# Moving one bias addition and one pair's LayerNorm pieces within the MLP of an adaLN block

## The chip, the cores and the metric

The kernel runs on one core of one Trainium2 chip. The metric is the time of one execution on the device in microseconds; several executions are timed and their median is given. Beside them one execution is recorded by the hardware profiler; its times are microseconds from the start of its span. Five engines work side by side, each through its own queue of instructions in order: PE (matmul, with its weight loads as PEld), DVE (vector), ACT (scalar), POOL (GpSimd) and SP, which here only starts DMAs.

## The reference

One transformer block over 2048 tokens of 640 features. Six vectors are made from a condition `c`, then attention and MLP each act on a LayerNorm that these vectors scale and shift:

```python
mod = (silu(c) @ w_mod).reshape(1, 6, 1, -1)          # sa, ca, ga, sb, cb, gb
h = layernorm(x) * (1 + ca) + sa
x = x + ga * A(h)                                     # linear attention, 32 heads of 20
h = layernorm(x) * (1 + cb) + sb
r = relu(h @ w1 + b1)                                 # 640 -> 1728
x = x + gb * ((r * r) @ w2 + b2)                      # 1728 -> 640
```

Everything is float32. Matmuls are done as sums of products of a rounded part ("hi") and the rest ("lo").

## The kernel before

The tokens stand in 16 tiles of 128, two tiles to a pair, so that the MLP goes over eight pairs, j = 0 to 7. A pair has seven steps n of two half steps. I call the half steps by pair and number: 2:4 is pair 2, half step 4, which is n = 2, first half. This is also the number `at` that the tables `LN_AT...` use. Pair 3 is the fourth pair.

In half step j:k PE computes `up`: 128 of the 1728 hidden features for both tiles of the pair (L79, tile `up`). ACT adds `b1` and takes the relu into `ft` (L1268), DVE squares it (L1269), ACT and DVE make its hi and lo parts `ra` (L1292, L89). After `up` PE does its share of the products with `w2` for the step before (tiles `acc`, `acc3x`). From pair 2 on these products are done in a scheme with fewer products, for which DVE also makes four sums (L1283), split into `rs` (L1308), and which reads prepared weights from a `ring` of four tiles. POOL fetches these from HBM, one fetch for each product that frees a tile (`t_fetch`, L1378). The prepared weights are made during pairs 1 and 2: `t_load` loads two rows `traw`, `t_sums` subtracts, `t_split` splits and SP stores them; the sixth and last of these (`t_split(5)`, tile `tst_end`) stands in half step 2:5.

From pair 2 on both `up` outputs of a step lie in one PSUM bank, so the next `up` starts only once the relu of the one before has read its half. The last hidden chunk (half step 13) has 64 features, and DVE reads its half of the bank, too (L1273), then makes the square (L1274).

While PE works on pair j, the other engines prepare pair j + 1: `load_x1` loads `XM`, `ln_dealt` takes two sums (L1538) and two sums of squares (L1543) on ACT, with POOL's small operations after each two (L1540, L1545 to L1547); then copies of the statistics (L1555, L1557), the normalisation of a second, "dealt" copy `XX` of the tokens (L1562, loaded by eight small DMAs in `load_dealt`), DVE's transposes `turn` (L1104), and in `t2` (L374, L375, and a subtraction on DVE) the scaled and split `H2` for the next pair's `up`. At which half step each piece stands is written in the tables: `ln` has seven places (two sums, two sums of squares, the copies, two normalisations), `dealt` and `turn` are the loads and transposes, and the keys 9 to 13 are the parts of `t2`.

When a pair's products are done, the next pair's half steps 0 and 1 read them out (`end`, L1440), and `finish` adds the residual rows `XR` (L1437) and stores. `residual` loads `XR` at n = 5, and `add_bias` adds `gb * b2` to them, two additions of 128 x 640.

Rows of 640 floats come from a pool "s1" of five buffers; a new row waits until one of the five has been read for the last time. One is held to the end by the last piece of `w1`. The others serve `traw`, `XR`, and, for pair 3 alone, the dealt rows, because the buffer that other pairs use for them is taken:

```python
BUFS = {"k": 2, "s1": 5, "s2": 2, "s3": 3, "s4": 5}
places += [lambda nm: row("s1", nm)[:, None, :].bitcast(F32R)]
```

The order of instructions on PE, DVE, ACT and POOL is as the program is written within a pair's region (pairs 0, 1 and 2 to 7 are three regions); between regions, and on SP in pair 1, a planner sets the order.

Of the kernel before, what the change touches and what calls it, by code (L numbers as in the profile page):

```python
# [52 lines left out]
def kernel(  # L53
# [64 lines left out]
    def row(tag, name):  # L118
        return (pc if tag in ("s3", "s4") else mem).tile([P, D], F32, tag=tag, name=name, bufs=BUFS[tag])
# [598 lines left out]
    for t in range(2, NT - 2):  # L718
        j, i = divmod(t, 2)
# [341 lines left out]
    XX = {}  # L1061
# [26 lines left out]

    def load_dealt(j):
        if j == 3:  # L1090
            XX[j] = [row("s1", f"xx{j}_{i}") for i in range(3)]
        else:
            h = ht(f"xx{j}", j).rearrange("p d s n -> p (d s n)").bitcast(F32)
            XX[j] = [h[:, D * i : D * i + D] for i in range(3)]
        for i in range(2):
            for q in range(4):
                nc.sync.dma_start(
                    XX[j][i][32 * q : 32 * q + 32].rearrange("t (a c) -> t a c", a=4),
                    A1[2 * j + i][:, 160 * q : 160 * q + 160].rearrange("(a t) c -> t a c", a=4),
                )  # L1100
# [328 lines left out]
    def add_bias(j, i):  # L1429
        add(XR[j, i], XR[j, i], bb)  # L1430
# [5 lines left out]
    def add(o, a, b):  # L1436
        nc.vector.tensor_tensor(o, a, b, op=ALU.add)  # L1437

    def by_gate(o, a, c):
        nc.vector.tensor_tensor(o, a, gb_b[:, c], op=ALU.mult)  # L1440
# [14 lines left out]
    def end(j, r, i, c):  # L1455
        o = Y[j][i][:, c]
        if j >= PLAIN:
            add(o, o, acc(j, r)[1])
        else:
            by_gate(o, acc(j, r)[1], c)  # L1460
# [43 lines left out]

    LN_AT0 = {"load": 0, "dealt": 1, "ln": (2, 3, 3, 4, 5, 7, 8), "turn": (8, 9), 10: (0, 1), 11: (2, 3), 12: (4,)}
    LN_AT1 = {"load": 0, "dealt": 1, "ln": (2, 2, 3, 3, 4, 5, 7), "turn": (6, 8), 9: (0, 1), 11: (2, 3), 12: (4,)}
    LN_AT2 = {"load": 0, "dealt": 5, "ln": (5, 5, 6, 6, 7, 8, 9), "turn": (9, 10), 11: (0, 1), 12: (2, 3), 13: (4,)}
    LN_AT = {"load": 0, "dealt": 1, "ln": (4, 4, 5, 5, 6, 7, 8), "turn": (8, 9), 10: (0, 1), 11: (2, 3), 12: (4,)}
    PREPS = iter([1, 3] + [2, 1, 2, 2, 1, 2] + [1, 1] + [1, 2])

# [20 lines left out]
    def ln_dealt(j):  # L1531
        sm = small([P, 2], "sm", f"smb{j}")
        rn = tiny.tile([P, 2, 2], F32, tag="rn", name=f"rn{j}", bufs=1)
        ra = tiny.tile([P, 4, 2, 2], F32, tag="rna", name=f"rna{j}", bufs=1)
        sq, nb = rn[:, :, 0], rn[:, :, 1]
        junk = XX[j][2]
        for i in range(2):
            nc.scalar.activation(junk, XM[j][:, i], AF.Identity, accum_out=sm[:, i : i + 1])  # L1538
            if i:
                nc.gpsimd.tensor_scalar(sm, sm, -1.0 / D, None, op0=ALU.mult)  # L1540
            yield
        for i in range(2):
            nc.scalar.activation(junk, XM[j][:, i], AF.Square, bias=sm[:, i : i + 1], accum_out=rn[:, i, 0:1])  # L1543
            if i:
                nc.gpsimd.tensor_scalar(sq, sq, 1.0 / D, EPS, op0=ALU.mult, op1=ALU.add)  # L1545
                nc.gpsimd.tensor_tensor(sq, sq, mhalf, op=ALU.pow)
                nc.gpsimd.tensor_tensor(nb, sm, sq, op=ALU.mult)  # L1547
            yield
        for a in range(4):
            for q in range(4):  # L1550
                o, v = ra[32 * q : 32 * q + 32, a], rn[32 * a : 32 * a + 32]
                if j <= PLAIN:
                    nc.gpsimd.tensor_copy(o, v)
                elif q % 2:
                    nc.scalar.activation(o, v, AF.Copy)  # L1555
                else:
                    nc.vector.tensor_copy(o, v)  # L1557
        yield
        for i in range(2):
            for a in range(4):  # L1560
                x = XX[j][i][:, 160 * a : 160 * a + 160]
                nc.scalar.activation(x, x, AF.Identity, bias=ra[:, a, i, 1:2], scale=ra[:, a, i, 0:1])  # L1562
            yield

    def layer(j, at, part=None):
        todo = {1: LN_AT0, PLAIN: LN_AT1, PLAIN + 1: LN_AT2}.get(j, LN_AT)
        if j == NB:
# [21 lines left out]
    for j in range(NB):  # L1589
        if j <= PLAIN:  # L1590
            if j:
                by_hand.__exit__(None, None, None)
            by_hand = tc.manual_schedule(engines={ET_.PE, ET_.DVE, ET_.Activation, ET_.Pool} | ({ET_.SP} if j != 1 else set()))
            by_hand.__enter__()
        for n in range(NP):
            down = lambda k: prev and (down_plain if plain(*prev) else down_pair)(*prev, k)
            twice = not plain(j, n)
            m = NP * j + n - NP - 1
            if (j, n) == (NB - 1, NP - 1):
                for k in range(2):  # L1600
                    up(j, 2 * n + k)
                    split_a(j, n, (k,))
                break
            done = j - 1 if j and prev else None
            up(j, 2 * n)
            if prev and not plain(*prev):
                split_s(*prev)
            down(0)
            if j < PLAIN:
                layer(j + 1, 2 * n, None if j else 0)  # L1610
            if 0 < m < NP - 2:
                t_split(m - 1)
            if m == -1:
                t_load(0)
            if (j, n) == (PLAIN, 0):
                t_fetch(4)
            if j >= PLAIN:
                if n == 5 + (j == PLAIN) - (j == NB - 1):
                    for i in range(2):
                        add_bias(j, i)  # L1620
                layer(j + 1, 2 * n)
            prep(next(PREPS, 0))
            if j == 0:
                layer(j + 1, 2 * n, 1)
            if n == 0 and j:
                if j - 1 >= PLAIN:
                    first_combos(j - 1)
                else:
                    Y[j - 1] = [row("s2", f"y{j - 1}_{i}") for i in range(2)]
                for r, i, c in (("3", 0, R), ("2", 0, L)):  # L1630
                    end(j - 1, r, i, c)
            if n == 1 and j:
                gate(j - 1, 0)
                if j != PLAIN:
                    finish(j - 1, j < PLAIN)
            if n == 1 and j == PLAIN:
                finish(j - 1, 0)
            if n == 2 and j == PLAIN:
                t_sums(NP - 2)
            if n == (2 if j > PLAIN else 1) and j:  # L1640
                gate(j - 1, 1)
            if n == (5, 5, 5, 3)[min(j, 3)]:
                residual(j)
            for i in range(2):
                if n == 6 and j == 0:
                    add_bias(j, i)
            if j == NB - 1 and n == 1:
                for k in range(NP - LAST, NP - 1):
                    plain_load(k)
            if j == NB - 1 and n == 3:  # L1650
                for k in range(NP - LAST, NP - 1):
                    plain_split(k)
            if j == NB - 1 and n == NP - 2:
                for i in range(2):
                    by_gate(Y[j][i], Y[j][i], slice(0, D))
                    add(Y[j][i], Y[j][i], XR[j, i])
            up(j, 2 * n + 1)
            if j >= PLAIN and n == 0:
                down(1)
            split_a(j, n)  # L1660
            if twice:
                sums(j, n)
            if j < PLAIN or n:
                down(1)
            if m == NP + 1:
                t_split(NP - 2)
            ahead = (j, n) == (0, 3)
            if ahead:
                layer(j + 1, 2 * n + 1)
            prep(next(PREPS, 0))  # L1670
            if n == 0 and j:
                end(j - 1, "4", 1, L)
                end(j - 1, "x", 1, R)
            if n == (2 if j > PLAIN else 1 if j == PLAIN else 0) and j:
                finish(j - 1, j >= PLAIN)
            if not ahead:
                layer(j + 1, 2 * n + 1)
            if (j, n) == (0, 4):
                nc.vector.tensor_tensor(bb, bb, gb_b, op=ALU.mult)
            if 0 <= m < NP - 2:  # L1680
                t_sums(m)
            if m == NP - 2:
                t_split(m - 1)
            if 0 < m + 1 < NP - 1:
                t_load(m + 1)
            if m == NP - 1:
                for i in range(2):
                    add_bias(j - 1, i)
            if j == NB - 1 and n == NP - LAST:
                first_combos(j)  # L1690
            prev = j, n
# [60 lines left out]
```

## Time and profile before

| | |
|---|---|
| median of 3 runs | 762.3 us (761.41 to 762.86) |
| profiled execution | 760.53 us, span 758.8 us |
| busy: PE, PEld, DVE, ACT, POOL | 751.5, 732.2, 605.3, 456.7, 168.7 us |
| granted TensorE clock | 1.000 |
| MLP | from about 387 us to the end |

A row of the timeline gives the start in us, the duration, the engine, the line of the program, the operation, output and input tiles with their shape, the number of instructions merged into the row, and in brackets the idle time of the engine ahead of it with what ended it. Starts are those of the first instruction of a row, and instructions on one engine can overlap a little.

### The profile page before, as it was taken

The page shows a single profiled execution, that of the slowest core. Times are in us where ns is not written, and L with a number is a line of the kernel's source. Part 1 is how long each engine was busy: PE and PEld are TensorE (multiplying, and loading weights), DVE is VectorE, ACT ScalarE, POOL GpSimd, SP SyncE. Part 2 cuts the span into 40 slices and gives each one's busy share as a digit, 9 for nine tenths or more (in the row PEclk, how much of TensorE's full clock was granted, in tenths as well). Part 3 has the DMA queues.
Part 4 walks back from the last instruction along what each step waited for, and adds up shares of the span by engine and source line. Part 5 has one row for each costly group of instructions (what it writes and reads, how often), then busy time and mean ns, then how long its engine had stood idle before and what let it go on. Part 6 is the DMA issues. An engine that isn't in the chain of part 4 may idle for free.

```text
span 758.8 us, 15386 instructions
## 1 busy us (share of the span) xinstructions
PE 751.5 (99%) x5898; PEld 732.2 (96%) x5898; DVE 605.3 (80%) x1121; ACT 456.7 (60%) x1054; POOL 168.7 (22%) x349
## 2 busy tenths in 40 slices
PE   9999999999999999999999999999999999999997
PEld 9999999999999988998999999999999999999997
DVE  6598997988999899998655868777777776777766
ACT  5767666677853365555777656466474756647431
POOL 3001101011100247543413020132221313213110
PEclk9999999999999999999999999999999999999999
DMA  9812431342332354644886555997677777767461
GB/s 328 329 57 83 139 105 54 105 137 103 137 105 94 94 167 149 164 105 105 208 206 213 141 191 212 283 273 214 186 206 209 205 196 201 207 177 216 125 182 36
DMA packets 57778, 126.04 MB, mean 166 GB/s; under 512 B 7324, under 2 KB 15265, under 8 KB 57705
## 3 DMA queue, kind: packets, MB, share of 16 engines
q1 hardware_dynamic: 37554, 78.75, 31.5%
q0 software_dynamic: 17568, 41.00, 21.9%
q10 hardware_dynamic: 2583, 5.30, 1.8%
q8 instruction: 46, 0.75, 0.4%
q14 instruction: 27, 0.22, 0.1%
HBM read 100.29 MB, written 29.89 MB: 172 GB/s over the span
## 4 chain that ended last, share of the span: by engine, by line
PE 87%; DVE 9%; ACT 3%; issue 1%; POOL 0%; DVEq 0%; POOLq 0%
PE up L79 22%; PE acc L79 16%; PE pq L79 9%; PE pk L79 9%; PE pv L79 9%; PE pwo L79 6%; PE acc3x L79 4%; PE kvp L455 3%; PE te L925 1%; DVE dn L883 1%; DVE scr L881 1%; DVE ezb L905 1%; PE ta L363 1%; DVE ot L89 1%; PE foldq L281 1%
## 5 line engine op out<-in xcount | busy, mean ns | idle before, releaser
L79 PE MATMUL up<-h,w 128*128 128x256 f32 x1640 | 204.6, 277 | 1.2 <-ACT ft L1268 0.9
L79 PEld LDWEIGHTS up<-h,w 128*128 128x128 f32 x1640 | 196.3, 188 | 2.1 <-ACT ft L1268 1.2
L1268 ACT ACTIVATE ft<-up,b_t 128x256 f32<-128x256 f32 x104 | 48.8, 470 | 97.4 <-PE up L79 97.2
L79 PE MATMUL acc<-w,ra 128*128 128x384 f32 x452 | 97.9, 336 | 0.6 <-DVE ra L89 0.6
L79 PE MATMUL pwo<-wo,ot 128*128 128x256 f32 (+3 forms) x512 | 80.6, 312 | 0.1
L1269 DVE TENSOR_TENSOR ft<-ft 128x256 f32<-128x256 f32 x104 | 43.9, 422 | 44.2 <-ACT ft L1268 42.8
L79 PEld LDWEIGHTS pwo<-wo,ot 128*128 128x128 f32 (+1 forms) x512 | 74.4, 188 | 3.2 <-issue 2.7
L79 PE MATMUL pq<-wq,hT 128*128 128x384 f32 (+1 forms) x480 | 75.1, 312 | 0.0
L79 PEld LDWEIGHTS acc<-w,ra 128*128 128x128 f32 x452 | 72.8, 188 | 1.9 <-DVE ra L89 1.7
L79 PE MATMUL pk<-wk,hT 128*128 128x384 f32 (+1 forms) x480 | 72.7, 309 | 0.0
L79 PE MATMUL pv<-wv,hT 128*128 128x384 f32 (+1 forms) x480 | 71.6, 307 | 0.0
L79 PEld LDWEIGHTS pq<-wq,hT 128*128 128x128 f32 x480 | 71.0, 188 | 0.6 <-issue 0.2
L79 PEld LDWEIGHTS pk<-wk,hT 128*128 128x128 f32 x480 | 70.5, 188 | 0.4 <-issue 0.2
L79 PEld LDWEIGHTS pv<-wv,hT 128*128 128x128 f32 x480 | 70.0, 188 | 0.0
L89 DVE TENSOR_TENSOR ra<-ft,ra 128x384 fp32r<-128x384 f32 (+2 forms) x86 | 36.8, 449 | 32.5 <-ACT ra L1292 19.9
L1378 POOL DMA_DIRECT2D ring_a<-td_a x34 | 18.5, 544 | 116.7 <-PE acc L79 105.6
L1292 ACT ACTIVATE ra<-ft 128x384 fp32r<-128x384 f32 x48 | 25.2, 526 | 28.4 <-DVE ft L1269 22.3
L79 PE MATMUL acc3x<-w,ra 128*128 128x256 f32 x231 | 39.8, 279 | 0.0
L79 PEld LDWEIGHTS acc3x<-w,ra 128*128 128x128 f32 x231 | 37.3, 188 | 0.2 <-DVE ra L89 0.2
L1283 DVE TENSOR_TENSOR ft<-ft 128x128 f32<-128x128 f32 x136 | 33.4, 287 | 1.2
L446 DVE TENSOR_REDUCE sk<-ek 128x64 f32<-128x1280 f32 x16 | 23.7, 1484 | 12.4 <-ACT ek L441 10.8
L889 POOL TENSOR_TENSOR dn<-dn,rs_q 128x32 f32<-128x32 f32 x32 | 20.1, 629 | 60.1 <-DVE dn L883 59.8
(274 smaller groups left out, 1454.1 us busy)
## 6 DMA issues: line engine op xcount, KB each, us to landing
ring_c<-td_c POOLq DMA_DIRECT2D x34, 384.0 KB, 3.9
ring_a<-td_a POOLq DMA_DIRECT2D x34, 384.0 KB, 3.4
ring_b<-td_b POOLq DMA_DIRECT2D x34, 256.0 KB, 3.4
esp<-eq SPq DMA_DIRECT2D x12, 640.0 KB, 3.1
el<-esp SPq DMA_DIRECT2D x12, 640.0 KB, 4.3
rw<-in_w SPq DMA_DIRECT2D x23, 320.0 KB, 3.5
wm<-in_w_mod SPq DMA_DIRECT2D x20, 320.0 KB, 3.4
xb<-in_x SPq DMA_DIRECT2D x8, 640.0 KB, 4.1
```

Source lines behind the costliest of these rows:

```text
L79: nc.tensor.matmul(o, a, b, start=first and i == 0, stop=last and i == len(terms) - 1, skip_group_check=skip,)
L89: (eng or nc.vector).tensor_tensor(out_lo, full, hi.bitcast(F32), op=ALU.subtract)
L281: nc.tensor.matmul(p[g // 3][:, (g % 3) * 120 : (g % 3) * 120 + n], r, bd_t[:120, g * 120 : g * 120 + n], start=True, stop=True,)
L363: nc.tensor.transpose(p[:, i * P : (i + 1) * P], src, ident)
L446: nc.vector.tensor_reduce(s, heads(flat(e)), axis=AX.X, op=ALU.add)
L455: nc.tensor.matmul(kvp[g // 4][64 * c : 64 * c + 64, a : a + 2 * n].rearrange("p (s n) -> p s n", s=2), v[:, u], e[:, :, o : o + n], start ...
L889: nc.gpsimd.tensor_tensor(dn[:, s], dn[:, s], rs[:, 1 - s], op=ALU.mult)
L1268: nc.scalar.activation(r, p, AF.Relu, bias=b1_t[:, f : f + 1])
L1269: nc.vector.tensor_tensor(r, r, r, op=ALU.mult)
L1283: nc.vector.tensor_tensor(t[:, o], t[:, a], t[:, b], op=op)
L1292: nc.scalar.activation(a[:, 0, :3], t[:, :3], AF.Copy)
L1378: nc.gpsimd.dma_start(RING[j, n, r], TD[n][r].bitcast(F32R))
```

## The change

It does three things. The bias of pair 0 (`add_bias(0, i)`) is added in half step 1:0, after the first two `end` products of pair 0 are read out, and no longer in 0:12. For pair 3, the tables move: the two sums from 2:5, 2:5 to 2:2 and 2:3, the two sums of squares from 2:6, 2:6 to 2:4, 2:4, the copies from 2:7 to 2:6, the normalisations from 2:8 and 2:9 to 2:7 and 2:8, the transposes from 2:9 and 2:10 to 2:8 and 2:9, the parts of `t2` from 2:11, 2:12, 2:13 to 2:10, 2:11, 2:12, and the dealt loads from 2:5 to 2:4. And the row that the sums write and nobody reads (`junk`), which for pair 3 was the third of the dealt rows, is a row "s1" of its own that is taken at the first sum.

```diff
 def load_dealt(j):
     if j == 3:
-        XX[j] = [row("s1", f"xx{j}_{i}") for i in range(3)]
+        XX[j] = [row("s1", f"xx{j}_{i}") for i in range(2)]
...
-LN_AT2 = {"load": 0, "dealt": 5, "ln": (5, 5, 6, 6, 7, 8, 9), "turn": (9, 10), 11: (0, 1), 12: (2, 3), 13: (4,)}
+LN_AT2 = {"load": 0, "dealt": 4, "ln": (2, 3, 4, 4, 6, 7, 8), "turn": (8, 9), 10: (0, 1), 11: (2, 3), 12: (4,)}
...
 def ln_dealt(j):
-    junk = XX[j][2]
+    junk = row("s1", f"junk{j}") if j == 3 else XX[j][2]
...
             for r, i, c in (("3", 0, R), ("2", 0, L)):
                 end(j - 1, r, i, c)
+            if j == 1:
+                for i in range(2):
+                    add_bias(0, i)
...
-        for i in range(2):
-            if n == 6 and j == 0:
-                add_bias(j, i)
```

## The prediction

> **What bounds the kernel now.** I read the page first, then PE's waits, then the timeline of each engine where a wait falls.
>
> ```profile
> span 758.8 us, 15386 instructions
> ...
> PE 751.5 (99%) x5898; PEld 732.2 (96%) x5898; DVE 605.3 (80%) x1121; ACT 456.7 (60%) x1054; POOL 168.7 (22%) x349
> ```
>
> ```profile
> PE up L79 <- ACT ft L1268: 0.9, 1, 0.9
> PE acc L79 <- DVE ra L89: 0.6, 2, 0.4
> PE up L79 <- ACT h L375: 0.2, 1, 0.2
> ```
>
> PE is the bound: 751.5 of 758.8 us. The change touches no PE instruction, so it can only win what PE loses waiting, and only in those places where a moved instruction holds it up. The list of PE's waits names three such entries in the MLP, 1.7 us together. That is too little, because a late start also stretches the matmuls beside it. So I measure the loss by the distance from one `up` to the next, against the same distance where nothing waits.
>
> ```profile
> 432.29 1.86 PE L79 MATMUL up<-h,w 128*128 128x256 f32 x15
> ...
> 434.91 0.44 PE L79 MATMUL acc<-w,ra 128*128 128x384 f32 x1 [0.41 <-DVE ra L89]
> ...
> 435.90 0.62 PE L79 MATMUL acc<-w,ra 128*128 128x384 f32 x2 [0.18 <-DVE ra L89]
> ...
> 436.58 1.86 PE L79 MATMUL up<-h,w 128*128 128x256 f32 x15
> ...
> 492.95 1.86 PE L79 MATMUL up<-h,w 128*128 128x256 f32 x15
> ...
> 499.45 1.86 PE L79 MATMUL up<-h,w 128*128 128x256 f32 x15
> ...
> 503.74 1.99 PE L79 MATMUL up<-h,w 128*128 128x256 f32 x15 [0.87 <-ACT ft L1268]
> ...
> 507.11 1.86 PE L79 MATMUL up<-h,w 128*128 128x256 f32 x15
> ...
> 523.36 1.30 PE L79 MATMUL up<-h,w 128*128 128x256 f32 x10
> ...
> 526.27 1.63 PE L79 MATMUL up<-h,w 128*128 128x256 f32 x12
> ...
> 530.36 1.86 PE L79 MATMUL up<-h,w 128*128 128x256 f32 x15
> ...
> 569.25 1.30 PE L79 MATMUL up<-h,w 128*128 128x256 f32 x10
> ...
> 571.93 1.86 PE L79 MATMUL up<-h,w 128*128 128x256 f32 x15
> ...
> 575.06 1.86 PE L79 MATMUL up<-h,w 128*128 128x256 f32 x15
> ```
>
> An undisturbed half step of pair 2 takes 3.25 us (two of them from 492.95 to 499.45). The short one, k = 13, takes 2.68, and the next, k = 0, 3.13 (569.25, 571.93, 575.06, pair 4's start; pair 1's start does the same plain products). Against these there are three losses:
>
> - A, half step 1:0: 436.58 - 432.29 = 4.29, loss 4.29 - 3.13 = **1.16**.
> - B, 2:6 and 2:7: 4.29 and 3.37 (499.45, 503.74, 507.11), loss 1.04 + 0.12 = **1.16**.
> - C, 2:13 and 3:0: 2.91 and 4.09 (523.36, 526.27, 530.36), loss 0.23 + 0.96 = **1.19**.
>
> **The bias of pair 0.** The two additions and what follows them:
>
> ```profile
> 432.32 1.55 DVE L1437 TENSOR_TENSOR xr<-xr,bb 128x640 f32<-128x640 f32 x2
> 433.79 0.41 DVE L1273 TENSOR_TENSOR ft<-up,ft 64x256 f32<-64x256 f32 x1
> ...
> 434.58 0.48 DVE L89 TENSOR_TENSOR ra<-ft,ra 128x128 fp32r<-128x128 f32 x2
> ...
> 438.99 0.43 DVE L1269 TENSOR_TENSOR ft<-ft 128x256 f32<-128x256 f32 x1 [1.32 <-ACT ft L1268]
> ```
>
> ```profile
> 431.97 0.47 ACT L1272 ACTIVATE ft<-up,b_t 64x256 f32<-64x256 f32 x1
> ...
> 434.19 0.47 ACT L1268 ACTIVATE ft<-up,b_t 128x256 f32<-128x256 f32 x1 [1.21 <-PE up L79]
> 434.69 0.42 ACT L1302 ACTIVATE ra<-ft 64x256 fp32r<-64x256 f32 x1
> ```
>
> The input of L1273 was ready at 432.44 (431.97 + 0.47), but DVE added the bias from 432.32 and came to L1273 at 433.79. Without the additions L1273 starts at about 432.45, 1.34 sooner, and the `ra` parts at 433.24 instead of 434.58. PE comes to the products that use them once the `up` of 432.29 is through, 1.86 later, at about 434.15. So it no longer waits, and A goes: -1.16. One thing can keep half of it. L1302 stands behind the relu at 434.19 although the program has it before, because at the border of two regions the planner chose. If that order stays, L1302 can't come before 434.19, and the 64-row part that ended PE's second wait (435.90) comes at most 434.69 - 434.19 = 0.5 sooner, so at least 0.66 of A stays. But L1302's input will be there 1.34 sooner, ahead of the relu's, so I take the order to turn and the full 1.16.
>
> At the new place the additions fill the 1.32 us in which DVE is idle before the square at 438.99. They take 1.55, so the square comes 0.23 later relative to PE, and `ra`, which is made from it, too. Before PE reads that `ra` it has another `up` of 1.86 to do, so I take 0 and keep 0.23 as the upper end. Were the idle time not there, all 1.55 would push on.
>
> **The sums leave 2:5.** ACT there, and where the pieces go:
>
> ```profile
> 491.61 0.47 ACT L1268 ACTIVATE ft<-up,b_t 128x256 f32<-128x256 f32 x1 [2.21 <-PE up L79]
> ...
> 494.91 0.47 ACT L1268 ACTIVATE ft<-up,b_t 128x256 f32<-128x256 f32 x1 [1.81 <-PE up L79]
> ...
> 498.11 0.48 ACT L1268 ACTIVATE ft<-up,b_t 128x256 f32<-128x256 f32 x1 [2.21 <-PE up L79]
> ...
> 501.63 0.74 ACT L1538 ACTIVATE xx<-xm 128x640 f32<-128x640 f32 x1 [0.58 <-DVE tst_end L89]
> ...
> 502.50 0.74 ACT L1538 ACTIVATE xx<-xm 128x640 f32<-128x640 f32 x1
> ...
> 503.23 0.46 ACT L1268 ACTIVATE ft<-up,b_t 128x256 f32<-128x256 f32 x1
> ...
> 505.05 0.83 ACT L1543 ACTIVATE xx<-xm,smb 128x640 f32<-128x640 f32 x1
> ```
>
> B is this: in 2:5 ACT has the last weight split, then waits 0.58 for a row that DVE still reads (the junk row was a `traw` buffer), then does both sums, and the relu that the next `up` needs runs at 503.23 instead of about 501.3 (499.45 + 1.86). With the sums gone the split alone fits. -1.16.
>
> In the new places ACT is idle before the relu for 2.21, 1.81 and 2.21 us. A sum takes 0.87 (501.63 to 502.50); a sum of squares is 0.09 longer (0.83 against 0.74), two of them 1.92. So by length all fit: 0.87 in 2.21, 0.87 in 1.81, 1.92 in 2.21. The copies, normalisations and transposes move one place and find the same half steps; C's cover stays as it was.
>
> But the first sum must have a row, and there is none. Five buffers: one held by `w1`, and by 2:2 two `XR` rows of pair 1 and the last two `traw` rows, which live until 2:5.
>
> ```profile
> 491.35 0.82 DVE L1437 TENSOR_TENSOR y<-y,xr 128x640 f32<-128x640 f32 x1
> ```
>
> The first row to come free is the `XR` row that `finish(1, 0)` reads last, at 491.35 + 0.82 = 492.17. The sum stands on ACT ahead of the relu of 2:3, and that relu gates the `up` of 2:4; the squares, `ra` and `rs` queue behind it, too. The times of B give the rest: sum to relu 0.73 (502.50 to 503.23), relu to `up` 0.51 (503.23 to 503.74). The `up` of 2:4 starts at 492.17 + 0.03 + 0.73 + 0.51 = 493.44 instead of 492.95, a loss of 0.49, and after such a wait the half step is 0.12 longer as in B: **+0.61** (D). The bounds are 0, if the row came earlier, and B's 1.16; I take 0.61, since every part is a row.
>
> **The hand-over to pair 3.** In C the `up` of 3:0 waited twice: for L1273, which reads its bank, and for the last part of `H2`, made in 2:13.
>
> ```profile
> 525.14 0.76 DVE L89 TENSOR_TENSOR h<-xm,h 128x256 fp32r<-128x256 f32 x2
> 525.81 0.41 DVE L1273 TENSOR_TENSOR ft<-up,ft 64x256 f32<-64x256 f32 x1
> ```
>
> L1273 ended at 526.22 and `up` began at 526.27; undisturbed it would have begun at 523.36 + 2.68 = 526.04. After the change 2:12 has one `h` subtraction, not two, before L1273. That is 0.33 sooner (0.76 for two, 0.43 for one): 525.89, 0.15 ahead of the need. The last `H2` part, which held up 3:0 by 0.96, is then made a half step earlier. So C goes: -1.19. The additions of pair 2's bias stay in 2:12, so the cover is thin; if 0.15 isn't enough, at most C's first 0.23 returns.
>
> **Loads.** The eight dealt loads now stand on SP ahead of the stores of `tst_end`. The first four get the row of `finish(1, 1)`, the others the junk row after the squares. They delay no store that POOL needs soon, but they run beside POOL's ring fetches, which also have POOL's LayerNorm operations ahead of them.
>
> ```profile
> DMA to landing us min/median/max: 2.8/3.4/6.2
> ```
>
> ```profile
> ring_b<-td_b POOLq DMA_DIRECT2D x2, 256.0 KB, 3.8
> ```
>
> ```profile
> 499.00 0.55 POOL L1378 DMA_DIRECT2D ring_b<-td_b  x1 [1.67 <-PE acc L79]
> ...
> 507.14 0.19 POOL L1547 TENSOR_TENSOR rn<-smb,rn 128x2 f32<-128x2 f32 x1
> ```
>
> The first row is ring_b over the whole kernel, the second the stretch from 496 to 512 us, where the dealt loads run now: 3.8 us from issue to landing, 0.4 over the median. The fetch at 499.00 serves the product two half steps later, so it has about 2 x 3.25 = 6.5 us, more than the slowest took. POOL's last LayerNorm operation ends 507.33 - 505.05 = 2.28 after the second sum of squares starts; that start is now about 0.9 ahead of a relu at 498.6 (498.11 and D), so POOL is free at 497.7 + 2.28 = 500.0, and this fetch goes 1.0 later at most, with 5.5 left. Cost taken: 0; what lies beyond it is a rival. The Trainium skill (DMA: Bandwidth & Descriptors, Issuing engines are not separate DMA queues) says that DMAs started by different engines run on the same 16 DMA engines and interleave, which speaks against putting these loads under other fetches. The trace agrees with its 3.8 against 3.4, and by the rule the excess moves with the loads and grows with what else runs.
>
> **Sum.** -1.16 - 1.16 + 0.61 - 1.19 = **-2.9 us**. The profiled execution took 760.53 (span 758.8, 1.73 around it): I expect 757.6. It lies 1.77 under the median of the runs, 762.3; with the same distance the median becomes **759.4**. 0.2% of it, about what a measurement can tell from no change, is 1.5 us.
>
> **Rivals.**
> 1. The hand-over isn't cleared. DVE's work of 2:12 and 2:13 stays late, C's 1.19 returns, and the gain is 1.7: 760.6. With the 0.66 of A it is 1.05: 761.25, no change. For it speaks that the margin is 0.15; against it that the part that cost 0.96 has a whole half step more.
> 2. Slower: the ring becomes the bound. Two ring_b fetches, from 2:5 and 2:7, run under the dealt loads, the `tst_end` stores and the `XR` loads. One that lands later than 6.5 us after its tile came free stops PE by the difference. The sign turns where both take 6.5 + 2.9 / 2 = 8.0 us; at 8.7 they cost 4.4, and the time is 763.8. The largest landing of ring_b, 6.2, and 1.0 for POOL make 7.2, which speaks against it, the denser traffic for it. It is what the rule of the page comes to if the transfers pile up.
> 3. The change does not do what it says: the junk row's wait eats more than D, up to B's 1.16, because B has only moved from one half step to another. Then the gain is 2.35: 759.95.
>
> **How the numbers follow.** The forecast, with rival 3 in it, from D = 0 (gain 3.5, 758.8) to the 0.66 of A kept (gain 2.24, 760.05): 0.70, of which rival 3 is 0.10. Rival 1: 0.15, of which 0.08 is still over 1.5 us faster and 0.07 not. Rival 2: 0.15, split by how late the fetches are into 0.02 faster, 0.05 the same, 0.08 slower. Faster 0.70 + 0.08 + 0.02 = 0.80, same 0.07 + 0.05 = 0.12, slower 0.08. The range goes from 758.4 (its lower end less 0.4 for the spread of a median, as the runs lie 761.41 to 762.86) to 761.4, which takes in rival 1 and the mild part of rival 2.
>
> **What would show it.** Right: no wait of PE for `ra` near 434 us, and the additions directly after `end`; the first sum's ACT idle ended by DVE's L1437 `y`, and the `up` of 2:4 about 0.5 late; 3.25 us from 2:6 to 2:7; 2.7 and 3.1 at 2:13 and 3:0. Wrong: `up` waits longer than 0.6 in 2:4, PE waits for ring tiles between 2:6 and 2:9, or L1302 still stands behind the relu.

## The result and the profile after

The changed kernel takes 759.08 us (median of 6 runs, 758.10 to 760.11), against 762.58 for the kernel before beside it (761.19 to 762.91): ratio 0.996 [0.9947, 0.9972]. A second comparison gave 758.97 against 761.89: 0.9955 [0.9939, 0.997]. So the change makes the kernel about 3 us faster, and the prediction, 759.4 with a range from 758.4 to 761.4, holds. The ratios here are not the quotients of the two medians beside them: by the ratio the change gains 3.0 and 3.4 us, by the medians 3.5 and 2.9.

The profiled execution tells less: 759.95 us, only 0.58 under the 760.53 of before. The page after, its first lines:

```profile
span 758.1 us, 15384 instructions
...
PE 752.0 (99%) x5898; PEld 732.9 (97%) x5898; DVE 605.0 (80%) x1121; ACT 457.1 (60%) x1054; POOL 169.1 (22%) x349
```

No engine's busy time has moved by more than 0.7 us. That fits a change that takes nothing away and only moves work. What PE waited for after, over the whole span:

```profile
PE warm L630 <- POOL bdc L156: 1.1, 1, 1.1
PE up L79 <- ACT ft L1268: 0.3, 1, 0.3
```

The first stands in the profile before, too, ahead of the MLP. In the MLP, the waits for `ra` and for `h` are gone, and of the 0.9 for the relu 0.3 is left, in another place. The starts of `up` in the timeline of PE after show each place:

```profile
434.16 1.86 PE L79 MATMUL up<-h,w 128*128 128x256 f32 x15
...
437.30 1.86 PE L79 MATMUL up<-h,w 128*128 128x256 f32 x15
...
490.43 1.87 PE L79 MATMUL up<-h,w 128*128 128x256 f32 x15
...
494.17 1.99 PE L79 MATMUL up<-h,w 128*128 128x256 f32 x15 [0.34 <-ACT ft L1268]
...
497.56 1.87 PE L79 MATMUL up<-h,w 128*128 128x256 f32 x15
...
500.80 1.86 PE L79 MATMUL up<-h,w 128*128 128x256 f32 x15
...
504.06 1.87 PE L79 MATMUL up<-h,w 128*128 128x256 f32 x15
...
507.30 1.86 PE L79 MATMUL up<-h,w 128*128 128x256 f32 x15
...
510.56 1.87 PE L79 MATMUL up<-h,w 128*128 128x256 f32 x15
...
513.57 0.62 PE L79 MATMUL acc<-ring_b,rs 128*128 128x256 f32 x3
514.03 1.87 PE L79 MATMUL up<-h,w 128*128 128x256 f32 x15
...
523.79 1.30 PE L79 MATMUL up<-h,w 128*128 128x256 f32 x10
...
526.47 1.90 PE L79 MATMUL up<-h,w 128*128 128x256 f32 x15
...
529.64 1.86 PE L79 MATMUL up<-h,w 128*128 128x256 f32 x15
```

| half step | us before | us after | us undisturbed |
|---|---|---|---|
| 1:0 | 4.29 | 3.14 | 3.13 |
| 2:3 | 3.24 | 3.74 | 3.25 |
| 2:4 | 3.26 | 3.39 | 3.25 |
| 2:6 | 4.29 | 3.26 | 3.25 |
| 2:7 | 3.37 | 3.24 | 3.25 |
| 2:9 | 3.25 | 3.47 | 3.25 |
| 2:13 | 2.91 | 2.68 | 2.68 |
| 3:0 | 4.09 | 3.17 | 3.13 |

A, B and C are gone, D is there, and 2:9 lost 0.22, which is new. Now the same instructions set side by side in time. Half step 1:0 starts 1.87 us later than before (434.16 against 432.29), 1:1 starts 0.72 later (437.30 against 436.58), and 3:1 starts 0.72 sooner (529.64 against 530.36). The span ends 0.7 sooner. So where the change works it gained 1.87 + 0.72 = 2.6 us, and this profiled execution had lost 1.9 before it came there: 0.56 ahead of 0:3 (it starts at 395.30, not 394.74), and the rest later in pair 0, which is shown with the scatter, further down.

### The profile page after: what moved, and what is told of

The parts are those of the page before. It is cut to its first block, busy times and chain, and to the rows that moved or that the text cites. A ratio compares the mean times of both kernels' runs of the same rounds, so it can differ in the third digit from the quotient of the medians.

```text
span 758.1 us, 15384 instructions
## 1 busy us (share of the span) xinstructions
PE 752.0 (99%) x5898; PEld 732.9 (97%) x5898; DVE 605.0 (80%) x1121; ACT 457.1 (60%) x1054; POOL 169.1 (22%) x349
## 4 chain that ended last, share of the span: by engine, by line
PE 87%; DVE 8%; ACT 2%; DMA 1%; issue 1%; POOL 0%; DVEq 0%; ACTq 0%; POOLq 0%
PE up L79 22%; PE acc L79 17%; PE pq L79 9%; PE pk L79 9%; PE pv L79 9%; PE pwo L79 6%; PE acc3x L79 4%; PE kvp L455 3%; DMA rw<-in_w 1%; PE te L925 1%; DVE dn L883 1%; DVE scr L881 1%; DVE ezb L905 1%; PE foldk L281 1%; PE ta L363 1%; DVE ot L89 1%
```

## The experiments

Each ran beside the kernel before on the same chip. The first four share one set of runs of it (median 761.6), the other four another, on another chip (761.89). Where a gain is given without more, it goes by the ratio. The theory was that of the prediction: four separate places, A, B, C and D, whose sizes add up. The rivals were that the parts depend on each other, that the row for `junk` costs nothing or much more, and that the earlier loads trade one wait for another.

**The bias alone.** Only `add_bias(0, i)` moves; the tables and the junk row are those of before.

```diff
+            if j == 1:
+                for i in range(2):
+                    add_bias(0, i)
-            for i in range(2):
-                if n == 6 and j == 0:
-                    add_bias(j, i)
```

> The kernel before with one edit: the bias of pair 0 is added in 1:0 after the first two products are read out. My theory takes the three losses as separate: only A goes, 1.16 us, so the ratio to the kernel before is 0.9985, and in the profile the distance from the up of 1:0 to that of 1:1 is 3.13 instead of 4.29, while 2:6 keeps its 4.29 and 3:0 its 4.09. Rival: what PE wins at 1:0 is given back later because pairs 1 and 2 wait for something with a time of its own (a load, the weights that are prepared there); then the ratio is 1.000 and a later half step is longer than it was. Second rival: the order of ACT's L1302 and the relu stays, and only 0.5 of A goes.

Measured: 760.57 us, ratio 0.9983 [0.9973, 0.9994], which is 1.3 us less (1.0 by the medians). The `up` of 1:0 and of 1:1 in its timeline:

```profile
432.96 1.86 PE L79 MATMUL up<-h,w 128*128 128x256 f32 x15
...
436.09 1.86 PE L79 MATMUL up<-h,w 128*128 128x256 f32 x15
```

3.13 us: A is gone, while 2:6 (4.29), 2:13 (2.91) and 3:0 (4.11) keep their losses. No half step from 1:1 to 2:5 is longer than before by over 0.01, so nothing of it is given back there. A is the bias's alone.

**The tables and the junk row alone.** The bias of pair 0 stays in 0:12; all else is the change.

```diff
-LN_AT2 = {"load": 0, "dealt": 5, "ln": (5, 5, 6, 6, 7, 8, 9), "turn": (9, 10), 11: (0, 1), 12: (2, 3), 13: (4,)}
+LN_AT2 = {"load": 0, "dealt": 4, "ln": (2, 3, 4, 4, 6, 7, 8), "turn": (8, 9), 10: (0, 1), 11: (2, 3), 12: (4,)}
...
-    junk = XX[j][2]
+    junk = row("s1", f"junk{j}") if j == 3 else XX[j][2]
```

> The kernel before with the other part: the new table for pair 3, two dealt rows, and the junk row of its own; the bias of pair 0 stays in 0:12. Theory: B and C go and D comes, -1.16 - 1.19 + 0.61 = -1.74 us, ratio 0.9977; A stays with 4.29 from 1:0 to 1:1. Together with the run of the bias alone this gives the whole -2.9. Rival: the two parts need each other (the bias also shifts when the rows come free), then the sum of the two is smaller than the whole by over 0.5 us.

Measured: 760.37 us, 0.998 [0.9968, 0.9992], 1.5 us less (1.2 by the medians). Half step 1:0 again takes 4.30. Of the other pair, 2:3 loses 0.49 and 2:4 loses 0.21, and B and C are gone. The two halves together make 0.0017 + 0.0020 = 0.0037, or 2.8 us; the whole measured 0.0040 and 0.0045, well inside the sum of their intervals. By the medians the halves make 2.3, and the whole 3.5 and 2.9, so the times alone don't exclude the rival that the parts need each other. The half steps speak against it: each loss goes or comes with its own part, A, B and C at their full size and D at 0.70 for 0.63.

**A row of its own for the junk that nothing else holds.** From the change, the junk row becomes a small extra tile of bf16, which has no earlier reader.

```diff
-    junk = row("s1", f"junk{j}") if j == 3 else XX[j][2]
+    junk = p3.tile([P, D], mybir.dt.bfloat16, tag="junk", name=f"junk{j}", bufs=1) if j == 3 else XX[j][2]
```

> The kernel after with one edit: what the sums of pair 3 write and nobody reads goes to a buffer of its own outside the five rows (as bfloat16, since there is room for 1280 bytes only; the sums themselves stay float32). Nothing is left out. Theory: the first sum then waits for nothing, starts at once behind the rs split of 2:2, the relu of 2:3 is on time, and D goes: the up of 2:4 comes 3.25 us after that of 2:3 instead of 3.74, 0.6 us less than the kernel after. Rival: the sum itself is too long for that place (DVE's or ACT's work in 2:2 is the cause, not the row); then the 3.74 stays and the time is that of the kernel after.

Measured: 758.32 us, 0.9954 [0.994, 0.9968]. ACT around the first sum, in its timeline:

```profile
490.76 0.72 ACT L1538 ACTIVATE junk<-xm 128x640 bf16<-128x640 f32 x1
...
493.06 0.47 ACT L1268 ACTIVATE ft<-up,b_t 128x256 f32<-128x256 f32 x1 [1.49 <-PE up L79]
```

The sum runs straight behind `rs`, the relu waits only for PE, and 2:3 and 2:4 take 3.24 and 3.26 us. So D comes from the row and from nothing else: the sum itself fits, as the prediction's lengths had it. The time agrees with 0.6 us of further gain but doesn't show it: its interval overlaps that of the change.

**The hand-over late, as before.** From the change, only the transposes and the parts of `t2` go back.

```diff
-LN_AT2 = {"load": 0, "dealt": 4, "ln": (2, 3, 4, 4, 6, 7, 8), "turn": (8, 9), 10: (0, 1), 11: (2, 3), 12: (4,)}
+LN_AT2 = {"load": 0, "dealt": 4, "ln": (2, 3, 4, 4, 6, 7, 8), "turn": (9, 10), 11: (0, 1), 12: (2, 3), 13: (4,)}
```

> The kernel after with the last places of the table put back: the transposes of pair 3 in 2:9 and 2:10, the parts of t2 in 2:11, 2:12 and 2:13; sums, copies, normalisations and loads stay early. Theory: C returns with both its waits, 0.23 at 2:13 and 0.96 at 3:0, so 1.2 us more than the kernel after, and nothing else moves. Rival: C was a consequence of B (work pushed late by the sums in 2:5), then C stays away and the time is that of the kernel after.

Measured: 760.33 us, 0.9981 [0.997, 0.9992], 1.4 us less than before, where the whole change has 3.0 and 3.4. PE's timeline at the hand-over, 2:13, 3:0 and 3:1:

```profile
523.24 1.30 PE L79 MATMUL up<-h,w 128*128 128x256 f32 x10
...
526.15 1.68 PE L79 MATMUL up<-h,w 128*128 128x256 f32 x12
528.00 0.96 PE L79 MATMUL up<-h,w 128*128 128x256 f32 x3 [0.16 <-ACT h L375]
...
530.26 1.93 PE L79 MATMUL up<-h,w 128*128 128x256 f32 x15
```

2.91 and 4.11: C is back in full, with its wait for `h`. This is what rival 1 of the prediction would have looked like.

**The change itself again.** It was run beside the next three, for a second profile.

> The kernel after, unchanged, once more, as the reference of this set on the same chip. Theory: 2.9 us less than the kernel before, ratio 0.9962, with A and C gone and the up of 2:4 about 0.5 late. The wait for a ring tile in 2:9 that the first profile has (0.2 us) should not be there each time, and the losses of pair 0, half steps 0:4 to 0:10, should be other ones than in the first profile, since nothing of the change stands there.

Measured: 758.97 us, 0.9955 [0.9939, 0.997]. D is the same to the hundredth (2:3 takes 3.74 and 2:4 3.39); the 0.22 of 2:9 is not there.

**Both sums in 2:3.** From the change, the first sum goes one half step later, behind the second one's place, when its row is free.

```diff
-LN_AT2 = {"load": 0, "dealt": 4, "ln": (2, 3, 4, 4, 6, 7, 8), "turn": (8, 9), 10: (0, 1), 11: (2, 3), 12: (4,)}
+LN_AT2 = {"load": 0, "dealt": 4, "ln": (3, 3, 4, 4, 6, 7, 8), "turn": (8, 9), 10: (0, 1), 11: (2, 3), 12: (4,)}
```

> The kernel after with both sums of pair 3 in 2:3, in place of one in 2:2 and one in 2:3; the junk row stays one of the five. Theory: in 2:3 the row of finish(1, 0) has long been free, so the first sum waits for nothing; two sums take 1.74 us where ACT is idle for 1.81, the relu of 2:4 is late by 0.1 at most and that is covered, D goes: 0.6 us less than the kernel after. Rival: two sums in one half step are what made B, so the loss moves to 2:5 (its up later than 3.25 after that of 2:4) and the time is that of the kernel after.

Measured: 758.18 us, 0.9942 [0.9929, 0.9956], the lowest of all. Beside the change on the same chip that is 0.8 us less by the medians (758.18 against 758.97), with intervals that overlap. D is gone: the first sum starts at 492.89, directly behind `ra`, and the relu of that half step waits 0.16 for PE. But 2:9 now loses 0.88, and 2:10 and 2:11 lose 0.09 and 0.08, which was not expected, and PE's waits have two entries in the MLP that are not in those of the change:

```profile
PE acc L79 <- DMA ring_a<-td_a: 0.2, 1, 0.2
PE acc L79 <- DMA ring_b<-td_b: 0.2, 1, 0.2
```

**The dealt loads where they were.** From the change, only the loads go back from 2:4 to 2:5.

```diff
-LN_AT2 = {"load": 0, "dealt": 4, "ln": (2, 3, 4, 4, 6, 7, 8), "turn": (8, 9), 10: (0, 1), 11: (2, 3), 12: (4,)}
+LN_AT2 = {"load": 0, "dealt": 5, "ln": (2, 3, 4, 4, 6, 7, 8), "turn": (8, 9), 10: (0, 1), 11: (2, 3), 12: (4,)}
```

> The kernel after with the dealt loads of pair 3 back in 2:5, behind the stores of the last prepared weights; the normalisations stay in 2:7 and 2:8. Theory: SP gets to the loads about 7 us later, at 505 and not at 498, the first four land at 510 to 513, and the normalisation of 2:7, which ACT begins at 507.4, holds ACT for 3 to 6 us; the relu of 2:8 waits behind it, and PE loses 2 to 5 us there. So the earlier loads are needed for the earlier places. Rival: the loads have room enough (they landed in 5 us with 9 to spare), then the time is that of the kernel after within 0.3 us.

Measured: 766.06 us, 1.0057 [1.0035, 1.0078]; 7.1 us more than the change, and slower than the kernel before. SP, then ACT, then PE in its timeline:

```profile
503.07 5.12 SPq L1097 DMA_DIRECT2D xx<-a  x8
...
512.03 1.75 ACT L1562 ACTIVATE xx<-xx,rna 128x160 f32<-128x160 f32 x4 [6.02 <-DMA xx<-a]
513.69 0.45 ACT L1268 ACTIVATE ft<-up,b_t 128x256 f32<-128x256 f32 x1
...
514.19 3.57 PE L79 MATMUL up<-h,w 128*128 128x256 f32 x15 [4.92 <-ACT ft L1268]
```

Behind the three stores of `tst_end` the eight loads go out from 503.07 on, where the change issues them from 497.82 (they stand ahead of those stores there). The normalisation of 2:7 waits 6.02 us for them, the relu stands behind it on ACT, and PE behind the relu for 4.92. So the earlier places of the LayerNorm work only with the earlier loads; the two are one edit. A loss of 2 to 5 us was expected, from the wait alone. The rest of the 7.1 is a second thing: the fifteen matmuls that follow took 3.57 us, not 1.86, told below.

**The junk tile and another order of the first row loads.** From the kernel with its own junk tile, the list of how many row preparations each half step of pair 0 gets is changed, to lessen the scatter there.

```diff
-    PREPS = iter([1, 3] + [2, 1, 2, 2, 1, 2] + [1, 1] + [1, 2])
+    PREPS = iter([1, 2] + [2, 2, 2, 2, 1, 2] + [1, 1] + [1, 2])
```

> The kernel after with the junk of pair 3's sums in a buffer of its own, and in pair 0 one of the three weight pieces of half step 0:1 moved to 0:2 (the list of pieces per half step begins 1, 2, 2, 2 and not 1, 3, 2, 1). The second edit is for the losses at 0:4, which differ from run to run (0.0 to 1.7 us): there ACT waits for a row of weights that SP loads late, and the relu behind it is late. Theory: with a half step more for that row the loss at 0:4 goes, 0.7 us on the average, and the spread of the times becomes smaller; with D gone as well, 1.2 us less than the kernel after. Rival: the row is only one of several that come late, and the loss moves to 0:6; then it is as good as the buffer alone, 0.5 us less than the kernel after.

Measured: 761.11 us, 0.9983 [0.9968, 0.9998], where the kernel that it was made from has 0.9954. It failed: 0:4 loses nothing, but 0:6 does. PE's longest wait there, and what ACT and SP did ahead of it:

```profile
PE acc L79 <- ACT ra L1292: 1.8, 1, 1.8
```

```profile
396.01 7.30 SPq L1097 DMA_DIRECT2D xx<-a  x8
403.42 0.36 SPq L1011 DMA_DIRECT2D rw<-in_w  x1
...
406.26 0.74 ACT L1018 ACTIVATE w<-rw 128x640 fp32r<-128x640 f32 x1 [1.86 <-DMA rw<-in_w]
```

One row load that used to go ahead of the eight loads of `xx` now stands behind them on SP, and they take it 7.30 us to issue. Half step 0:6 lost 3.59, more than the 2.59 that pair 0 had lost in all in the profile of the kernel with its own junk tile. A part of it is PE's clock, told at the end: six of the twelve runs show a mean granted clock of 0.995 to 0.997 and take 761.2 to 764.3 us, the other six 0.999 to 1.000 and 758.5 to 761.0. D, B and C stayed as in the kernel with its own junk tile.

## Why the prediction was right

**A, predicted -1.16, measured -1.15.** DVE and ACT after, at the border from pair 0 to pair 1, in the timeline:

```profile
434.36 0.42 DVE L1273 TENSOR_TENSOR ft<-up,ft 64x256 f32<-64x256 f32 x1
...
437.84 0.55 DVE L1440 TENSOR_TENSOR y<-acc,gb_b 128x384 f32<-128x384 f32 x1
438.30 1.55 DVE L1437 TENSOR_TENSOR xr<-xr,bb 128x640 f32<-128x640 f32 x2
```

```profile
435.26 0.42 ACT L1302 ACTIVATE ra<-ft 64x256 fp32r<-64x256 f32 x1 [0.40 <-DVE ft L1274]
436.06 0.48 ACT L1268 ACTIVATE ft<-up,b_t 128x256 f32<-128x256 f32 x1 [0.39 <-PE up L79]
```

L1273 starts 0.20 after the `up` of 1:0; before, it started 1.50 after it (433.79 against 432.29). L1302 now stands ahead of the relu, and waits for DVE only: the order at the border turned, so the 0.66 that could have stayed did not. The additions stand directly behind `end`, and no half step from 1:1 to 1:13 is more than 0.01 longer than before: their new place costs nothing, the value taken.

**B, -1.16, measured -1.16.** 2:6 and 2:7 went from 4.29 and 3.37 to 3.26 and 3.24.

**D, +0.61, measured +0.63.** DVE's last read of the row, and ACT behind it:

```profile
492.08 0.82 DVE L1437 TENSOR_TENSOR y<-y,xr 128x640 f32<-128x640 f32 x1
```

```profile
492.93 0.74 ACT L1538 ACTIVATE junk<-xm 128x640 f32<-128x640 f32 x1 [2.80 <-DVE y L1437]
...
493.67 0.46 ACT L1268 ACTIVATE ft<-up,b_t 128x256 f32<-128x256 f32 x1
```

Every link is as predicted: `y` ends at 492.90, the sum starts 0.03 later, the relu 0.74 after that (0.73 predicted), and the `up` 0.50 after the relu (0.51). ACT sat idle for 2.80 us in which the sum would have fitted, and the experiment with the junk tile shows that it does. Rival 3, D up to 1.16, did not come.

**C, -1.19, measured -1.15.** L1273 ahead of pair 3 after:

```profile
525.91 0.41 DVE L1273 TENSOR_TENSOR ft<-up,ft 64x256 f32<-64x256 f32 x1
```

It ends at 526.32, 0.15 ahead of the `up` at 526.47, exactly the margin that was worked out. The last part of `H2` no longer holds 3:0 up, either (3.17 for 4.09). So rival 1 stayed away; the 0.15 guards only C's first 0.23.

**The loads and rival 2: the mechanism was right, the bound a little too small.** The fetch of `ring_b` behind POOL's LayerNorm operations went at 501.24 where it had gone at 499.00. Of these 2.24 us, 1.35 is because all of pair 2 runs later in this execution (500.80 against 499.45 at 2:6), so 0.9 is the change's, under the 1.0 that was given. It came in time. The fetch after it didn't, quite. POOL's issue in the timeline, and `ring_b`'s landings in the stretch from 500 to 516 us:

```profile
506.85 0.53 POOL L1378 DMA_DIRECT2D ring_b<-td_b  x1 [1.69 <-PE acc L79]
```

```profile
DMA to landing us min/median/max: 4.2/4.9/6.7
```

506.85 + 6.7 = 513.55, and the product that reads it starts at 513.57 and is stretched from 0.50 to 0.62. The slack was put at 6.5 us and the slowest landing at 6.2; now it was 6.7, and 2:9 lost 0.22. The DMAs moved 391 GB/s while this fetch was under way, and 286 before. The same fetch, followed through the other profiles, shows the slack at work: it landed after 4.6 us before, after 6.0 to 6.4 in the five others with the earlier loads in which 2:9 lost nothing (the change again, the tables alone, the late hand-over, and both kernels with the junk tile), and after 7.3 with both sums in 2:3, where the loss was 1.05 (2:9 to 2:11). So with the earlier loads most of this slack was used up every time, and a loss came where 6.5 was passed. This is rival 2 in its mild form, far from the 2.9 at which the sign would turn. What makes the landing 6.0 in one execution and 6.7 in another stays open, since each is one profile.

**The sum.** Predicted -2.9, measured in the trace -1.15 - 1.16 + 0.63 - 1.15 + 0.22 = -2.6, and by the medians -3.5 and -2.9. The one term that was missing is the 0.22. That the median of 759.08 lies only 0.3 from the forecast is partly luck: the six runs go from 758.10 to 760.11, and the two comparisons differ by more than that. What the traces bear out is the four terms.

**The profiled execution, 757.6 predicted, 759.95 measured: this step failed.** I took the profile before as typical but for a fixed distance to the median. It wasn't. In pair 0, in work that the change leaves alone, some executions lose time. ACT in the profile after:

```profile
397.82 0.74 ACT L1018 ACTIVATE w<-rw 128x640 fp32r<-128x640 f32 x1 [1.58 <-DMA rw<-in_w]
```

The split waits for a row of weights, and the relu behind it comes late: 0:4 took 4.09 us (398.72 to 402.81), not 3.42. The rest, 0.62, was lost in 0:10. How much half steps 0:4 to 0:10 lost (single losses under 0.06 left out), how long SP took to issue the eight loads of `xx` that stand among the rows of weights, and how far each profiled execution lay from the median of its kernel's runs:

| profile of | lost in 0:4 to 0:10, us | SP's issue of eight loads, us | profiled less median, us |
|---|---|---|---|
| before | 0 | 6.86 | -2.05 |
| the tables alone | 0 | 6.24 | -0.76 |
| loads where they were | 0.14 | 6.89 | -0.62 |
| the bias alone | 0.76 | 7.07 | -0.40 |
| both sums in 2:3 | 0.69 | 7.07 | +1.07 |
| late hand-over | 1.30 | 7.83 | +0.34 |
| after | 1.31 | 7.75 | +0.87 |
| after, again | 1.78 | 7.93 | +1.41 |
| own junk tile | 2.59 | 8.95 | +1.51 |

The kernel with the other order of row loads is left out, since its loss there comes from its edit. The loss and the distance to the median rise together by and large, so the profile before was a lucky execution, and the median already held some of this loss. That is why the prediction of the median could be right with that of the profile wrong by 2.3. The loss also goes with the time that SP needed for the eight loads; which of the two brings on the other isn't shown. Whether the moved bias has any share isn't settled, either: the two profiles without any loss are of kernels that leave the bias in 0:12. Against a share speaks that SP issues the loads of this stretch in the same order in all nine, that the bias stood behind these half steps in the program, that one kernel with the moved bias lost only 0.14, and that the bias alone gave its 1.3 us (1.0 by the medians).

## What to carry to other kernels

Measure what a wait costs as the distance between the same instruction in successive rounds, against an undisturbed round: PE's listed waits here came to 1.7 us, and the distances to 3.5. When an instruction is moved earlier, its output buffer and its loads have to move as well; look up who reads that buffer last (here an idle 2.80 us on ACT and 0.63 on PE for a row that nobody reads), and move the load with its reader (7.1 us when it stayed behind). Before a profile is set against another, align the two where the change begins, and give the losses ahead of that place to the scatter until runs say otherwise.

Of the kernels run, the one with both sums in 2:3 is the fastest, 758.18 us, and beats the kernel before by its whole interval; that it beats the change, or the kernel with the junk tile (758.32), is not shown. One with the junk tile or the later sum and with the `XR` loads held back from the stretch of 2:5 to 2:9 was not tried.

## What the runs showed that was not expected

**Half speed after a long wait.** With the dealt loads back in 2:5, the fifteen matmuls behind PE's idle 4.92 us took 3.57 us instead of 1.86. The table of windows of that kernel (after the busy times of PE, PEld, DVE, ACT and POOL: the granted TensorE clock, the DMA share, GB/s):

```profile
509.00:514.00 5.00, 0.27 (x2) 0.00 (x0) 0.00 (x0) 1.97 (x5) 0.53 (x1) 0.73 1.31 252
514.00:517.00 3.00, 2.81 (x13) 2.81 (x14) 2.39 (x3) 2.42 (x6) 0.00 (x0) 0.50 0.68 243
517.00:518.00 1.00, 1.00 (x6) 1.00 (x6) 0.00 (x0) 0.20 (x1) 0.00 (x0) 0.50 0.00 0
518.00:521.00 3.00, 3.00 (x26) 3.00 (x25) 2.07 (x7) 0.80 (x2) 1.06 (x2) 0.98 0.28 65
```

A mean of 0.73 over 5 us is 2.7 us at 0.50; with the 4 us after it and 0.1 of the last row that is 6.8 us at half clock. So the wait cost nearly half as much again: 2:8 lost 5.10, and 2:9, in which PE waits for nothing, another 1.97. The kernel with the other order of row loads did the same after a wait of 1.82 us:

```profile
409.00:410.00 1.00, 0.75 (x3) 0.46 (x3) 0.76 (x2) 1.00 (x4) 0.89 (x3) 0.81 0.96 362
410.00:411.00 1.00, 1.00 (x5) 1.00 (x6) 0.95 (x2) 1.00 (x4) 0.92 (x3) 0.50 0.23 85
...
412.00:413.00 1.00, 1.00 (x7) 1.00 (x6) 0.69 (x1) 0.00 (x0) 0.89 (x3) 0.50 0.81 261
413.00:414.00 1.00, 1.00 (x10) 1.00 (x10) 0.00 (x0) 0.00 (x0) 0.82 (x5) 0.98 0.87 312
```

Here it is 0.4 + 3 = 3.4 us at half clock, half of what the other had. The Trainium skill (TensorE: Matmul & The Clock Gate, What's actually happening) says that the activity of TensorE is judged in free-running windows of about 3.4 us, and that the clock drops to half after an idle one. The trace agrees with the length, 3.4 us once and 6.8, twice that, the other time; it differs on what counts as idle, since 1.82 us of waiting were enough. A wait of 1.12 us (in 0:4 of the kernel with its own junk tile, whose clock stayed at 1.00 there) was not. These are two waits only: where between them the limit lies, and whether it also matters when the wait falls, is not shown.

**POOL's small operations took longer beside a busier DVE.** The two operations on `rn` in 2:5 after, and the longer of them before:

```profile
499.20 0.32 POOL L1545 TENSOR_SCALAR rn<-rn 128x2 f32<-128x2 f32 x1 [0.47 <-ACT junk L1543]
499.60 0.99 POOL L1546 TENSOR_TENSOR rn<-rn,mhalf 128x2 f32<-128x2 f32 x1
```

```profile
506.34 0.72 POOL L1546 TENSOR_TENSOR rn<-rn,mhalf 128x2 f32<-128x2 f32 x1
```

Before they took 0.18 and 0.72. In this stretch DVE now runs subtractions of `traw` and a square one after the other, and before it was idle in half of theirs. With both sums in 2:3, where DVE is busy in over half of theirs, they took 0.25 and 0.79. The Trainium skill (SBUF — State Buffer, Who interferes with whom) says that a DVE instruction with two inputs in SBUF contends with a GpSimd instruction that reads SBUF; the trace agrees, with 0.27 us on the longer of the two. No run here takes only DVE's work away. The two make 0.4 of the 0.9 us by which the change delayed the fetch at 501.24.
